# First half of attention in a two-layer MLP kernel: the values of both batches stand together ahead of both results, and the first weight block is loaded and converted later

## The chip, the cores and the metric

The kernel runs on one core of a Trainium2 chip. The metric is the device time of one execution in microseconds (us); less is better. The engines are TensorE (PE, whose weight loads show as PEld), VectorE (DVE), ScalarE (ACT), GpSimd (POOL) and SyncE (SP), which here only issues loads and stores.

## The reference

Three stages follow each other. Attention with a per-head decay runs over 2 batches, 8 heads, 768 tokens of width 64; its result, 1536 rows of 512, goes through a gated MLP of width 1536, and that result through a second MLP of width 768 with three branches. The reference's weights are 64-bit floats.

```python
for b in range(nb):                       # blocks of tokens
    intra = einsum('bhic,bhjc->bhij', qb, kb) * Dmask
    intra = einsum('bhij,bhjd->bhid', intra, vb)
    inter = einsum('bhid,bhde->bhie', qb * lam_pow, kv_state)
    out[:, :, sl] = intra + inter
    kv_state = lam_block * kv_state + einsum('bhsd,bhse->bhde', kb * rev_pow, vb)
x = out.transpose(0, 2, 1, 3).reshape(B * S, H * D)
y = ((x @ w_a) * (x @ w_b)) @ w_out
return maximum(maximum(y @ w1, y @ w2), y @ w3) @ w_out2
```

## The kernel before, in words

**Attention.** The tokens are cut into chunks of 128. `order` (L343) numbers the 12 chunks so that 2m and 2m + 1 are the same chunk of the two batches: `pair(m)`. The first half of the tokens is pairs 0, 1 and 2. Each chunk n goes through these helpers:

- `load` (L357): one 512 KB load for queries and keys (`aq`), one for keys and values in row order (`av`).
- `scores` (L367): on PE, query times key into two banks `s`; `masked` (L377): two DVE passes that multiply a bank by the decay table into `am`.
- `queries` and `keys` (L389, L393): one POOL pass each, which weights `aq` or `av` by the decay.
- `earlier` (L402): on PE, queries times the held state, into the banks `ob` (named `o` in rows). A pair of chunks shares these two banks.
- `within` (L414): on PE, `am` times the values, into the same banks `o`, added to what stands there.
- `update` (L427): on PE, keys times values into a bank `k`; `carry` (L440) takes it into the held state, `stt` in rows: one ACT copy after pair 0, four DVE passes (L448) after the others.
- `taken` (L458): ACT passes that copy the result out of `o`, into `x` (32-bit) and `xh` (the rounded part that PE multiplies with); `lows` (L469): two DVE passes that form the rest, `xl` = `o` - `xh`.

A tile is one unit to the dependency tracker, and both chunks of a pair write one pair of banks `o`. So in program order a `within` that follows a `taken` and a `lows` of the pair's other chunk waits until both have read the banks.

**Weights.** Weight blocks come as 64-bit floats, 1 MB each (`wr`). `converted` (L211) makes 32-bit floats of them in four passes: DVE L221, ACT L224 (`ws`), DVE L229, DVE L231. `up_pair` (L236) then splits the block into `hi` (ACT, L190) and `lo` = `w` - `hi` (DVE or POOL, L187). Block 0 and block 1 belong to the first two column groups of the first MLP; each is six such steps. A `Task` holds the steps of a block; `steps(task, n)` (L838) puts the next n steps into the program there and then, and a task that is on the list `pace.tasks` is also put forward by `pace.pump`, which looks at an estimate of each engine's clock whenever PE work is added. The engine of `lo` is picked by that estimate or named by the third argument of `steps`.

**First MLP.** `plain_group` (L557, matmuls at L567, bank `p`) multiplies `xh`, `xl` by `hi`, `lo` in three terms. Its first group needs `xh`, `xl` of pairs 0 to 2 of batch 0 and `hi`, `lo` of block 0. From there on the other three pairs of attention are threaded between the groups of layer 1 (L915 to L950).

**Order of the work.** The scheduler is off (`manual_schedule`, L744): each engine runs its instructions in the order of the program text, and a wait holds up all that stands behind it on that engine. SP issues loads in text order too. Nine matmuls on zeros (`keep_warm`, L759) open PE's work, and eight more stand between the scores of pair 0 and the first `within`.

Of the kernel before, what the change touches and what calls it, by code (L numbers as in the profile page):

```python
# [163 lines left out]
def decay_attention_gated_mlps(ctx: ExitStack, tc: tile.TileContext, qkv: bass.AP, lam: bass.AP, wup: bass.AP, wdown: bass.AP, out: bass.AP):  # L164
# [7 lines left out]
    pace = Pace()  # L172
# [7 lines left out]
    def bank(name):  # L180
        return pp.tile([128, 512], F32, tag="ps", name=name)
# [17 lines left out]
    def load_to(n):  # L199
        while state["raw"] <= min(n, len(items) - 1):  # L200
            m = state["raw"]
            kind, i = items[m]
            t = wp.tile([128, 1024], I64, tag="r", bufs=2, name=f"wr{m}")
            if kind == "up":
                nc.sync.dma_start(out=t, in_=wup[i])
            else:
                nc.sync.dma_start(out=t[:, 0:WB], in_=wdown[i])
            raw[m] = t
            state["raw"] += 1
# [24 lines left out]
    wop, wtask = {}, {}  # L234
# [67 lines left out]
    def open_to(what, m):  # L302
        if m < len(items):
            items_to(m)
            pace.open((what, m))
# [39 lines left out]
    am, sc, ob, kv, at = {}, {}, {}, {}, {"st": 0.0}  # L345
    xa, xh, xl = {}, {}, {}
# [4 lines left out]
    def arrive(us):  # L351
        state["dma"] += us
        return state["dma"]
# [3 lines left out]
    def load(n, *which):  # L357

        b, c = order[n]
        for i in which:  # L360
            of, name = ((aq, "aq"), (av, "av"))[i]
            of[n] = slot(f"{name}{n}")
            at[name, n] = arrive(1.3)
            s = slice(512 if i == 1 and c == NC - 1 else 0, 1024)
            nc.sync.dma_start(out=of[n][:, s], in_=qkv[b * NC + c, i, :, s])

    def scores(n):  # L367

        q, k = aq[n][:, 0:512], aq[n][:, 512:1024]
        sc[n] = [bank(f"s{n}_{i}") for i in range(2)]  # L370
        for a in range(NP):
            o = slice(128 * a, 128 * a + 128)
            for i in range(2):
                nc.tensor.matmul(sc[n][i][:, o], k[rows(i), o], q[rows(i), o], start=True, stop=True)  # L374
        pace.pe(0.9, at["aq", n])

    def masked(n):  # L377

        am[n] = slot(f"am{n}")
        for i in range(2):  # L380
            nc.vector.tensor_tensor(out=am[n][:, 512 * i:512 * i + 512], in0=sc[n][i], in1=decay[:, 4 * i:4 * i + 4].rearrange("p a i -> p (a i)"), op=ALU.mult)
            at["am", n] = pace.run("DVE", 512, pace.t["PE"])
        sc.pop(n)
# [9 lines left out]
    def keys(n):  # L393
        k, o = (av[n][:, x:x + 512].rearrange("p (h d) -> p h d", h=H) for x in (0, 1024))
        nc.gpsimd.tensor_tensor(out=o, in0=k, in1=decay[:, :, C - 1:C].to_broadcast([128, H, D]), op=ALU.mult)
        at["kd", n] = beside(512, at["av", n])
# [5 lines left out]
    def earlier(n):  # L402

        q = aq[n][:, 1024:1536]
        for w in range(2):
            for i in range(2):
                for x in range(2):
                    a = 2 * w + x
                    nc.tensor.matmul(  # L409
                        place(n, 4 * i + a), held[rows(i), n % 2, a], q[rows(i), 128 * a:128 * a + 128],  # L410
                        start=n % 2 == 0 and w == 0, stop=False, skip_group_check=True)
        pace.pe(0.5, max(at["qs", n], at["st"]))

    def within(n):  # L414

        v = av[n][:, 512:1024]
        for w in range(2):
            for i in range(2):
                for x in range(2):
                    a = 2 * w + x  # L420
                    h = 4 * i + a
                    nc.tensor.matmul(  # L422
                        place(n, h), v[:, 64 * h:64 * h + 64], am[n][:, 128 * h:128 * h + 128],
                        start=n == 0 and w == 0, stop=n % 2 == 1 and w == 1, skip_group_check=True)
        pace.pe(0.9, max(at["av", n], at["am", n]))

    def update(n):  # L427

        if n % 2 == 0:
            kv[n // 2] = bank(f"k{n}")  # L430
        v, k = av[n][:, 512:1024], av[n][:, 1024:1536]
        for a in range(NP):
            for i in range(2):
                h, o = 4 * i + a, 256 * (n % 2) + 64 * a
                nc.tensor.matmul(  # L435
                    kv[n // 2][rows(i), o:o + 64], k[:, 64 * h:64 * h + 64], v[:, 64 * h:64 * h + 64],
                    start=n % 2 == 0 and a == 0, stop=n % 2 == 1 and a == NP - 1, skip_group_check=True)
        pace.pe(0.5, at["kd", n])

    def carry(m):  # L440

        src = kv[m].rearrange("p (b a e) -> p b a e", b=B, a=NP)
        if m == 0:
            copy(held, src)
            at["st"] = pace.run("ACT", 512, pace.t["PE"])
        else:
            for a in range(NP):
                nc.vector.scalar_tensor_tensor(out=held[:, :, a], in0=held[:, :, a], scalar=ahead[:, a, C - 1:C], in1=src[:, :, a], op0=ALU.mult, op1=ALU.add)  # L448
                at["st"] = pace.run("DVE", 128, pace.t["PE"] if a == 0 else 0.0)
# [8 lines left out]
    def taken(n, *to):  # L458
        b, c = order[n]
        j = c // 3  # L460
        for x, name, dt in zip((xa, xh, xl), ("x", "xh", "xl"), (F32, F32R, F32R)):
            if (j, b) not in x and (j == 0 or x is xa):
                x[j, b] = slot(f"{name}{j}{b}", dt).rearrange("p (a i) -> p a i", a=KD)
        for x in to:
            for i in range(2):
                copy(tokens_of(x, n, i), result(n, i))
                at["x", n, i] = pace.run("ACT", 256, pace.t["PE"])

    def lows(n):  # L469
        for i in range(2):  # L470
            nc.vector.tensor_tensor(out=tokens_of(xl, n, i), in0=result(n, i), in1=rd(tokens_of(xh, n, i)), op=ALU.subtract)  # L471
            pace.run("DVE", 256, at["x", n, i])
# [271 lines left out]
    with tc.manual_schedule():  # L744
        nc.sync.dma_start(out=lams, in_=lam)
        for m in range(3):
            for i in range(2):
                for n in (2 * m, 2 * m + 1):
                    load(n, i)
                if m == i == 0:  # L750
                    load_to(0)
                    at["wr"] = arrive(2.6)
        warm = sttab[:, 768:1024].bitcast(BF16)
        nc.vector.memset(warm, 0.0)
        patterns()
# [3 lines left out]
        def keep_warm(n):  # L759
            for i in range(n):  # L760
                nc.tensor.matmul(ps, warm[:, 0:128], warm, start=True, stop=True)
# [76 lines left out]
        def steps(task, n, e=None):  # L838
            while n and task.next is not None:
                if e is None:  # L840
                    task.step(pace)
                else:
                    task.ready = pace.run(e, task.next[1], after=task.ready, kind=task.next[2])
                    task.move(e)
                n -= 1
                pace.gone(task)

        def pair(m):
            return 2 * m, 2 * m + 1
# [11 lines left out]

        open_to("conv", 0)
        open_to("split", 0)
        for n in pair(0):
            scores(n)
            masked(n)
        keep_warm(8)
        wtask[0].ready = at["wr"]
        steps(wtask[0], 5)
        for n in pair(0):  # L870
            keys(n)
        for f, m in ((queries, 1), (keys, 1), (queries, 2)):
            for n in pair(m):
                f(n)
        steps(wtask[0], 1, "POOL")
        for n in pair(2):
            keys(n)
        load_to(1)
        arrive(2.6)
        for i in range(2):  # L880
            for n in pair(3):
                load(n, i)
        for m in range(2):
            ob[m] = [bank(f"o{m}_{i}") for i in range(2)]
            if m > 0:
                for n in pair(m):
                    earlier(n)
            for n in pair(m):
                within(n)
                update(n)  # L890
                taken(n, xh, xa)
                if n < 3:
                    lows(n)
            carry(m)
            for n in pair(m + 1):
                scores(n)
                masked(n)
        for i in range(2):
            for n in pair(4):
                load(n, i)  # L900
        ob[2] = [bank(f"o2_{i}") for i in range(2)]
        for n in pair(2):
            earlier(n)
        for n in pair(2):
            within(n)
            taken(n, xh)
        lows(4)
        lows(3)
        lows(5)
        for n in pair(2):  # L910
            taken(n, xa)
        open_to("conv", 1)
        open_to("split", 1)
        operands(0)
# [130 lines left out]
```

## Time and profile before

| | us |
|---|---|
| runs without profile | 518.37, 518.88, 519.06 (median 518.88) |
| the profiled execution, its own time | 519.24 |
| its span, first to last instruction | 517.5 |
| PE busy in the span | 503.0 (97%) |
| DVE, ACT, POOL busy | 372.5, 213.2, 57.1 |
| stretch 0 to 35.4, before the first MLP matmul | 6.8% of the span |

The profile was taken in one execution. Its page gives busy times of each engine, the span in 40 slices of 12.9 us, and the chain of work that ended last; the trace behind it gives instructions in order of time, each with the idle time of its engine before it and what ended that. PE's busy time cannot tell how well PE is used: a matmul at a low clock is busy for longer. [...]

### The profile page before, as it was taken

The page shows a single profiled execution, that of the slowest core. Times are in us where ns is not written, and L with a number is a line of the kernel's source. Part 1 is how long each engine was busy: PE and PEld are TensorE (multiplying, and loading weights), DVE is VectorE, ACT ScalarE, POOL GpSimd, SP SyncE. Part 2 cuts the span into 40 slices and gives each one's busy share as a digit, 9 for nine tenths or more (in the row PEclk, how much of TensorE's full clock was granted, in tenths as well). Part 3 has the DMA queues.
Part 4 walks back from the last instruction along what each step waited for, and adds up shares of the span by engine and source line. Part 5 has one row for each costly group of instructions (what it writes and reads, how often), then busy time and mean ns, then how long its engine had stood idle before and what let it go on. Part 6 is the DMA issues. An engine that isn't in the chain of part 4 may idle for free.

```text
span 517.5 us, 7772 instructions
## 1 busy us (share of the span) xinstructions
PE 503.0 (97%) x3175; PEld 467.7 (90%) x3175; DVE 372.5 (72%) x555; ACT 213.2 (41%) x358; POOL 57.1 (11%) x50
## 2 busy tenths in 40 slices
PE   6589999999999999999999999999999999999997
PEld 3579999999999999997888888899999999998886
DVE  5655978879777778859958068697999998887000
ACT  2333254534443334445534166354464354433211
POOL 2836210111111111211000000000000000000000
PEclk9799999999999999999999999999999999999999
DMA  8994202022122212303424020202102211110311
GB/s 321 411 345 186 84 2 81 1 81 101 65 81 82 81 63 62 120 5 122 134 79 155 1 81 2 82 1 81 47 37 81 82 61 62 61 62 1 112 70 62
DMA packets 10260, 47.17 MB, mean 91 GB/s; under 512 B 1264, under 2 KB 1520, under 8 KB 7536
## 3 DMA queue, kind: packets, MB, share of 16 engines
q1 hardware_dynamic: 10224, 46.67, 24.5%
q8 instruction: 25, 0.41, 0.3%
q14 instruction: 11, 0.09, 0.1%
HBM read 43.52 MB, written 3.15 MB: 90 GB/s over the span
## 4 chain that ended last, share of the span: by engine, by line
PE 93%; DVE 3%; DMA 1%; ACT 1%; issue 1%; SPq 0%; DVEq 0%
PE yp L666 18%; PE zu L549 16%; PE zv L549 15%; PE out L720 10%; PE bu L549 8%; PE bv L549 7%; PE p L567 6%; PE xu L549 4%; PE xv L549 4%; PE o L422 2%; PE s L374 2%; DMA wr<-wup_dram 1%; PE o L409 1%; PE k L435 1%; DVE gl L187 1%
## 5 line engine op out<-in xcount | busy, mean ns | idle before, releaser
L187 DVE TENSOR_TENSOR lo<-w,hi 128x1024 fp32r<-128x1024 f32 (+1 forms) x39 | 47.5, 1217 | 11.5 <-ACT hi L190 11.5
L190 ACT ACTIVATE hi<-w 128x1024 fp32r<-128x1024 f32 (+1 forms) x40 | 38.2, 956 | 17.5 <-DVE w L231 7.7
L666 PE MATMUL yp<-gl,dh 128*128 128x512 f32 x108 | 42.0, 389 | 0.0
L666 PE MATMUL yp<-gh,dl 128*128 128x512 f32 x108 | 42.0, 389 | 0.0
L666 PE MATMUL yp<-gh,dh 128*128 128x512 f32 x108 | 42.0, 389 | 0.0
L598 POOL TENSOR_TENSOR g<-z1u,z6u 128x384 f32<-128x384 f32 x20 | 24.0, 1202 | 150.3 <-DVE z6u L580 150.3
L187 DVE TENSOR_TENSOR gl<-g,gh 128x512 fp32r<-128x512 f32 x36 | 24.6, 706 | 17.8 <-ACT gh L190 17.8
L187 DVE TENSOR_TENSOR w<-w 128x256 f32<-128x256 f32 (+1 forms) x57 | 29.7, 521 | 1.0
L229 DVE SCALAR_TENSOR_TENSOR w<-ws,w 128x1024 int32<-128x1024 int32 x21 | 26.5, 1261 | 3.1 <-ACT ws L224 3.0
L709 DVE COPY ob<-out 128x256 f32<-128x256 f32 x1 | 0.4, 424 | 38.4 <-PE out L720 38.4
L224 ACT ACTIVATE ws<-wr 128x1024 f32<-128x1024 f32 x21 | 24.1, 1147 | 6.6 <-DMA wr<-wup_dram 6.6
L231 DVE SCALAR_TENSOR_TENSOR w<-ws,w 128x1024 int32<-128x1024 int32 x21 | 26.3, 1254 | 0.3
L190 ACT ACTIVATE z6u<-zu 128x384 f32<-128x384 f32 x20 | 9.8, 492 | 38.2 <-PE zu L549 38.2
L190 ACT ACTIVATE gh<-g 128x512 fp32r<-128x512 f32 x36 | 21.2, 622 | 7.1 <-PE yp L666 7.1
L666 PEld LDWEIGHTS yp<-gh,dl 128*128 128x128 f32 x108 | 20.3, 188 | 4.2
L666 PEld LDWEIGHTS yp<-gh,dh 128*128 128x128 f32 x108 | 20.3, 188 | 4.2
L666 PEld LDWEIGHTS yp<-gl,dh 128*128 128x128 f32 x108 | 20.3, 188 | 4.2
L190 ACT ACTIVATE z7u<-zu 128x384 f32<-128x384 f32 x20 | 9.8, 492 | 34.3 <-PE zu L549 34.3
L422 PE MATMUL o<-am,av 128*64 128x128 f32 x192 | 14.1, 291 | 7.9 <-DVE xl L471 6.1
L221 DVE TENSOR_SCALAR w<-wr 128x1024 int32<-128x1024 int32 (+1 forms) x26 | 18.5, 713 | 2.9 <-DMA wr<-wup_dram 2.5
L549 PE MATMUL zu<-x1A,hi 128*128 128x384 f32 x80 | 20.3, 334 | 0.0
L549 PE MATMUL bu<-x0S,hi 128*128 128x384 f32 x80 | 20.3, 334 | 0.0
(202 smaller groups left out, 1450.0 us busy)
## 6 DMA issues: line engine op xcount, KB each, us to landing
wr<-wup_dram SPq DMA_DIRECT2D x21, 1024.0 KB, 4.8
wr<-wdown_dram SPq DMA_DIRECT2D x12, 768.0 KB, 4.4
aq<-qkv_dram SPq DMA_DIRECT2D x12, 512.0 KB, 10.0
av<-qkv_dram SPq DMA_DIRECT2D x10, 512.0 KB, 10.2
out_dram<-ob SPq DMA_DIRECT2D x11, 256.0 KB, 2.1
av<-qkv_dram SPq DMA_DIRECT2D x2, 256.0 KB, 4.3
out_dram<-ob SPq DMA_DIRECT2D x2, 128.0 KB, 1.7
lams<-lam_dram SPq DMA_DIRECT2D x1, 6.0 KB, 1.6
```

What stands on the lines that cost most here:

```text
L187: (nc.vector if e == "DVE" else nc.gpsimd).tensor_tensor(out=o, in0=a, in1=b, op=op)
L190: nc.scalar.activation(out=o, in_=a, func=AF.Copy)
L221: nc.vector.tensor_scalar(out=w, in0=low, scalar1=29, scalar2=None, op0=ALU.logical_shift_right)
L224: nc.scalar.activation(out=near, in_=high.bitcast(F32), func=AF.Copy, scale=2.0 ** -112)
L229: nc.vector.scalar_tensor_tensor(out=w, in0=near, scalar=3, in1=w, op0=ALU.logical_shift_left, op1=ALU.bitwise_or)
L231: nc.vector.scalar_tensor_tensor(out=w, in0=near, scalar=-0x80000000, in1=w, op0=ALU.bitwise_and, op1=ALU.bitwise_or)
L422: nc.tensor.matmul(place(n, h), v[:, 64 * h:64 * h + 64], am[n][:, 128 * h:128 * h + 128], start=n == 0 and w == 0, stop=n % 2 == 1 and w ...
L549: nc.tensor.matmul(ps, w, x, start=p in FIRST and i == 0, stop=i == len(todo) - 1, skip_group_check=p not in FIRST)
L567: nc.tensor.matmul(ps, w[:, 128 * k:128 * k + 128], x[:, k], start=m == 0, stop=m == 11)
L598: nc.gpsimd.tensor_tensor(out=ga[g.n][:, tokens(g.j, 0)], in0=g.z[1], in1=g.z[6], op=ALU.mult)
L666: nc.tensor.matmul(ps[e], w[:, cols], g, start=k == 0 and m == 0, stop=k == K1 - 1 and m == 2)
L720: nc.tensor.matmul(ps, a[:, o:o + 128], w[:, s], start=k == 0 and n == 0, stop=k == K2 - 1 and n == 2)
```

## The change

Only the first half of attention is written anew (pairs 0 to 2), in the body under `manual_schedule`, and the order of the first loads. Everything up to there, all helpers, and everything from `open_to("conv", 1)` (L912) on are as before. Block 0's task is taken off the list of tasks, so that only `steps` puts its passes into the program.

```diff
             for i in range(2):
                 for n in (2 * m, 2 * m + 1):
                     load(n, i)
-                if m == i == 0:
-                    load_to(0)
-                    at["wr"] = arrive(2.6)
+            if m == 0:
+                load_to(0)
+                at["wr"] = arrive(2.6)
...
+        first = wtask[0]
+        pace.tasks.remove(first)
+        first.ready = at["wr"]
         for n in pair(0):
             scores(n)
             masked(n)
-        keep_warm(8)
-        wtask[0].ready = at["wr"]
-        steps(wtask[0], 5)
-        for n in pair(0):
             keys(n)
-        for f, m in ((queries, 1), (keys, 1), (queries, 2)):
...
-        for m in range(2):
+        for m in range(3):
             ob[m] = [bank(f"o{m}_{i}") for i in range(2)]
             if m > 0:
                 for n in pair(m):
                     earlier(n)
+            if m < 2:
+                for n in pair(m + 1):
+                    queries(n)
+            if m == 0:
+                for n in pair(1):
+                    keys(n)
+            if m == 1:
+                steps(first, 1)
             for n in pair(m):
                 within(n)
-                update(n)
-                taken(n, xh, xa)
-                if n < 3:
-                    lows(n)
-            carry(m)
-            for n in pair(m + 1):
-                scores(n)
-                masked(n)
+            for n in pair(m):
+                taken(n, xh)
+            for n in pair(m):
+                lows(n)
+            if m < 2:
+                for n in pair(m):
+                    update(n)
+                if m == 1:
+                    steps(first, 1)
+                carry(m)
+                if m == 0:
+                    steps(first, 3)
+            for n in pair(m):
+                taken(n, xa)
+            if m == 1:
+                steps(first, 1, "POOL")
+                for n in pair(2):
+                    keys(n)
+                load_to(1)
...
+            if m < 2:
+                for n in pair(m + 1):
+                    scores(n)
+                    masked(n)
```

On the engines the change moves instructions in three places; apart from them, the eight matmuls that are gone, the load of block 0 (now behind both first `av` loads instead of ahead of them) and ACT's passes, the five engines run the same instructions in the same order as before.

PE, the results of pair 0 (`within` L422, `update` L435), before and then after; av_85 and av_87 were the values of chunks 0 and 1, they are now av_83 and av_85:

```order
L422 MATMUL o_0_196<-am_147,av_85 64x128 x2
L422 MATMUL o_1_197<-am_147,av_85 64x128 x2
...
L435 MATMUL k_206<-av_85 64x64 x8
L422 MATMUL o_0_196<-am_160,av_87 64x128 x2
L422 MATMUL o_1_197<-am_160,av_87 64x128 x2
...
L435 MATMUL k_206<-av_87 64x64 x8
```

```order
L422 MATMUL o_0_160<-am_142,av_83 64x128 x2
L422 MATMUL o_1_161<-am_142,av_83 64x128 x2
...
L422 MATMUL o_0_160<-am_156,av_85 64x128 x2
L422 MATMUL o_1_161<-am_156,av_85 64x128 x2
...
L435 MATMUL k_196<-av_83 64x64 x8
L435 MATMUL k_196<-av_85 64x64 x8
```

Both chunks' values now stand together, and both updates behind them; pair 1 moved in the same way.

DVE, from the decay tables to the decay passes (`am`) of pair 1, before and then after; w and lo belong to block 0, xl to the results of pair 0:

```order
L221 TENSOR_SCALAR w_142<-wr_83 128x1024
L229 SCALAR_TENSOR_TENSOR w_142<-ws_144,w_142 128x1024
L381 TENSOR_TENSOR am_147<-s_0_132,tables 128x512
...
L381 TENSOR_TENSOR am_160<-s_1_151,tables 128x512
L231 SCALAR_TENSOR_TENSOR w_142<-ws_144,w_142 128x1024
L187 TENSOR_TENSOR lo_173<-w_142,hi_172 128x1024
L471 TENSOR_TENSOR xl_217<-o_0_196,xh_216 128x2x128
...
L381 TENSOR_TENSOR am_260<-s_0_250,tables 128x512
```

```order
L381 TENSOR_TENSOR am_142<-s_0_132,tables 128x512
...
L381 TENSOR_TENSOR am_156<-s_1_147,tables 128x512
L471 TENSOR_TENSOR xl_184<-o_0_160,xh_183 128x2x128
...
L221 TENSOR_SCALAR w_214<-wr_87 128x1024
L229 SCALAR_TENSOR_TENSOR w_214<-ws_216,w_214 128x1024
L381 TENSOR_TENSOR am_233<-s_0_223,tables 128x512
...
L381 TENSOR_TENSOR am_246<-s_1_237,tables 128x512
L231 SCALAR_TENSOR_TENSOR w_214<-ws_216,w_214 128x1024
```

Two of block 0's DVE passes moved behind the `am` and `xl` of pair 0, ahead of the `am` of pair 1; the third moved behind these; `lo` left DVE.

POOL, from the queries of pair 2 on, before and then after; lo_460 is the `lo` of block 1, lo_271 that of block 0:

```order
L390 TENSOR_TENSOR aq_97<-aq_97,tables 128x512
L390 TENSOR_TENSOR aq_99<-aq_99,tables 128x512
L395 TENSOR_TENSOR av_101<-av_101,tables 128x512
L395 TENSOR_TENSOR av_103<-av_103,tables 128x512
...
L395 TENSOR_TENSOR av_194<-av_194,tables 128x512
L187 TENSOR_TENSOR lo_460<-w_438,hi_459 128x1024
```

```order
L390 TENSOR_TENSOR aq_97<-aq_97,tables 128x512
L390 TENSOR_TENSOR aq_99<-aq_99,tables 128x512
L187 TENSOR_TENSOR lo_271<-w_214,hi_270 128x1024
L395 TENSOR_TENSOR av_101<-av_101,tables 128x512
L395 TENSOR_TENSOR av_103<-av_103,tables 128x512
```

The `lo` of block 0 came to POOL, ahead of the keys of pair 2; that of block 1 left POOL for DVE, where it stands between the `am` and the state's passes of pair 3.

## Rows read from the trace of the kernel before

**Rows 1.** The page's 40 slices of 12.9 us: the granted clock in tenths.

```profile
PEclk9799999999999999999999999999999999999999
```

**Rows 2.** Busy time by stage: start:end length, PE, PEld, DVE, ACT, POOL, PEclk, DMA share, GB/s.

```profile
10.60:14.00 3.40, 1.78 (x32) 1.40 (x32) 3.40 (x6) 0.00 (x0) 3.40 (x3) 1.00 1.03 413
14.00:19.10 5.10, 0.00 (x0) 0.00 (x0) 3.98 (x4) 2.15 (x5) 5.10 (x4) 0.83 1.03 410
19.10:24.20 5.10, 5.04 (x54) 4.89 (x56) 1.26 (x4) 1.84 (x5) 5.07 (x5) 0.51 1.02 412
24.20:35.40 11.20, 10.12 (x208) 8.72 (x204) 6.62 (x14) 3.17 (x11) 4.66 (x4) 1.00 0.97 378
35.40:72.40 37.00, 36.35 (x483) 33.01 (x481) 27.51 (x48) 14.56 (x31) 13.66 (x9) 1.00 0.33 119
72.40:517.50 445.10, 441.51 (x2357) 415.58 (x2357) 324.37 (x469) 188.87 (x305) 24.05 (x20) 1.00 0.19 67
```

**Rows 3.** The chain of work that ended last, up to the first MLP: start, length, what.

```profile
11.29 2.39 DVE am L381 x4
...
19.16 1.98 PE o L422 x16
...
21.98 3.03 PE s L374 x32
...
29.56 0.46 PE k L435 x16
30.02 1.99 PE s L374 x32
...
33.04 0.83 PE o L422 x12
...
35.72 0.43 DVE xl L471
...
36.20 4.26 PE p L567 x23
```

**Rows 4.** PE in order of time: start, length, what, idle before and its end.

```profile
6.30 2.41 PE L374 MATMUL s<-aq 64*128 64x128 f32 x32
...
19.16 1.98 PE L422 MATMUL o<-am,av 128*64 128x128 f32 x16 [5.27 <-DVE xl L471]
```

**Rows 5.** DVE in order of time, in the same form.

```profile
8.87 0.69 DVE L221 TENSOR_SCALAR w<-wr 128x1024 int32<-128x1024 int32 x1 [2.46 <-DMA wr<-wup_dram]
10.06 1.23 DVE L229 SCALAR_TENSOR_TENSOR w<-ws,w 128x1024 int32<-128x1024 int32 x1 [0.50 <-ACT ws L224]
...
13.60 1.93 DVE L231 SCALAR_TENSOR_TENSOR w<-ws,w 128x1024 int32<-128x1024 int32 x1
...
18.69 0.74 DVE L471 TENSOR_TENSOR xl<-o,xh 128x256 fp32r<-128x256 f32 x2
...
49.73 1.12 DVE L448 SCALAR_TENSOR_TENSOR stt<-stt,tables,k 128x128 f32<-128x128 f32 x4 [3.54 <-PE k L435]
...
52.57 1.38 DVE L221 TENSOR_SCALAR w<-wr 128x1024 int32<-128x1024 int32 x1
54.06 2.12 DVE L229 SCALAR_TENSOR_TENSOR w<-ws,w 128x1024 int32<-128x1024 int32 x1
```

**Rows 6.** ACT (its first row) and POOL in order of time.

```profile
26.91 0.66 ACT L190 ACTIVATE xh<-o 128x256 fp32r<-128x256 f32 x2 [4.28 <-PE o L422]
...
13.19 3.48 POOL L390 TENSOR_TENSOR aq<-aq,tables 128x512 f32<-128x512 f32 x2
...
43.47 2.40 POOL L187 TENSOR_TENSOR lo<-w,hi 128x1024 fp32r<-128x1024 f32 x1 [11.82 <-ACT hi L190]
45.83 2.50 POOL L390 TENSOR_TENSOR aq<-aq,tables 128x512 f32<-128x512 f32 x2
```

**Rows 7.** SP's issue of pair 1's queries, and the first one's time to landing.

```profile
3.62 0.99 SPq L365 DMA_DIRECT2D aq<-qkv_dram x2
...
aq<-qkv_dram SPq DMA_DIRECT2D x1, 512.0 KB, 9.1
```

More of the change, by code (lines that the diff above doesn't have):

```diff
@@ L866, in decay_attention_gated_mlps @@
             masked(n)
-        keep_warm(8)
-        wtask[0].ready = at["wr"]
-        steps(wtask[0], 5)
-        for n in pair(0):
             keys(n)
-        for f, m in ((queries, 1), (keys, 1), (queries, 2)):
[L873 to L882, printed above, removed]
-        for m in range(2):
+        for m in range(3):
             ob[m] = [bank(f"o{m}_{i}") for i in range(2)]
@@ L887, in decay_attention_gated_mlps @@
                     earlier(n)
+            if m < 2:
[6 more added lines that the diff above has]
+                steps(first, 1)
             for n in pair(m):
                 within(n)
-                update(n)
-                taken(n, xh, xa)
-                if n < 3:
-                    lows(n)
-            carry(m)
-            for n in pair(m + 1):
-                scores(n)
-                masked(n)
+            for n in pair(m):
[17 more added lines that the diff above has]
+                load_to(1)
+                arrive(2.6)
+                for i in range(2):
+                    for n in pair(3):
+                        load(n, i)
+            if m < 2:
+                for n in pair(m + 1):
+                    scores(n)
+                    masked(n)
         for i in range(2):
@@ L900, in decay_attention_gated_mlps @@
                 load(n, i)
[L901 to L911, printed above, removed]
         open_to("conv", 1)
```

## The prediction

> **What bounds the kernel now.** I read the 40 slices first, then the busy times by stage, then the chain of waits, and last the engines in order of time. [...] The stages [rows 2] say where time can be won: after 72.4 us PE is busy for 441.5 of 445.1 us, from 35.4 to 72.4 for 36.35 of 37.0, all at full clock. Whatever starts these stages earlier moves the end by as much; nothing else in them is touched. Before 35.4 us it is otherwise: PE does nothing from 14.0 to 19.1, and from 19.1 to 24.2 it is busy at 0.51 of the clock.
>
> My landmark is the second matmul of the first MLP, at 36.20 us, the last that waits in this stretch (for `xl`); its chain is in [rows 3]. The wait of 5.27 us ahead of it belongs to the second chunk's `within` [rows 4]: it may not touch the banks `o` until the first chunk's `xl` has read them, and on DVE that `xl` stands behind block 0's third pass (13.60, 1.93 us) and `lo`, and starts only at 18.69 [rows 5]. So a weight block that no product needs before 36 us holds up attention, and the idle time is followed by a low clock: 16 matmuls of `within` in 1.98 us, scores of a pair in 3.03 against 1.99 later [rows 3].
>
> **The change, step by step.** I rebuild the chain to the landmark from rows, handing over between engines at about 0.04 us (from `xl`'s end at 36.15 to the matmul at 36.20, [rows 3]).
>
> 1. *Scores of pair 0* stay at 6.30, 2.41 us for 32 matmuls [rows 4]. The eight matmuls on zeros behind them go; PE then waited for `am`, which began only at 11.29 [rows 3], so by themselves they cost nothing. What they may do for the clock is a rival below.
> 2. *`am` of pair 0*, four passes, 2.39 us from the first start to the last end as the chain counts them [rows 3]. DVE was free from 6.4 (8.87 less the idle 2.46, [rows 5]) and now takes them first: from about 7.8, when half the scores are done, to 10.2. Before, they ended at 13.7.
> 3. *Values of both chunks* follow pass by pass; behind the last pass remain 12 matmuls, 0.83 us [rows 3]: 11.0. The values must have landed for it: they move ahead of the 1 MB block, and at 413 GB/s [rows 2] 1 MB is 2.5 us and 512 KB 1.3; the block now being the last ahead of the load that lands at 12.7 (step 5), the second chunk's values land at 8.9, the first's at 7.6. Updates, 2 x 0.46: 12.0.
> 4. *`xh`, then `xl`.* ACT passes are 0.38 long and 0.28 apart (two in 0.66, [rows 6]). I let `xl` begin after three of them, since it now stands behind both chunks' `xh`: 0.94, then four DVE passes, 2 x 0.74 less an overlap of 0.08 twice, 1.33. `xl` ends at 13.3.
> 5. *Scores of pair 1* need queries issued at 3.62 that land 9.1 us later, at 12.7 [rows 7], the second chunk's one load after that (1.3 us, 512 KB at the same rate): done at 15.0. This load does not move, since what is ahead of it in the queue has the same bytes as before.
> 6. *Block 0's first two DVE passes* now stand ahead of `am` of pair 1. Alone they take 0.69 and 1.23, while POOL works on them, 1.38 and 2.12 [rows 5]. POOL gets its four passes for pair 1 as the loads land, 1.3 us apart from 12.7 on, so I take the dear values, 3.5 us: 16.8. The passes are now what is late, by 1.8 us against the scores.
> 7. *`am` of pair 1* 2.39: 19.2. *Third pass of block 0*, between POOL's passes as before, 1.93: 21.1. `xl` of pair 1, 1.33: 22.5 (`within` ends at 20.0, so `xh` is there). State passes, four in 1.12, next one starting 0.08 before their end: 23.5 (the updates end at 21.0). `am` of pair 2, 2.39: 25.9; its scores (1.99, from 21.0) are done by 23.0.
> 8. *Values of pair 2*, 0.83, *three `xh`*, 0.94, *first `xl`*, 0.43, and three hand-overs, 0.12: the landmark comes at 28.3 instead of 36.2, **7.9 us earlier**.
>
> Costed at nothing: `lo` of block 0 on POOL, 2.40 alone [rows 6], with `hi` ready near 22.5 it is done by 25, ahead of the products; the keys of pair 2 that queue behind it end by 27, and their updates come only after 24 products (some 4.3 us from 36.20, [rows 3]). `lo` of block 1 on DVE stands where DVE idled 3.54 us for an update [rows 5]. Other loads keep their order; pair 3's land before 31 us at this rate and are needed 5 us after the landmark.
>
> The profiled execution took 519.24 us, 1.7 more than its span, and 0.36 more than the median 518.88 of the runs. 519.24 - 7.9 is 511.3 for an execution like it; against the median I say **511.0**.
>
> **Bounds of what I can't see.** Step 6 and 7's three passes never stood in this place. Cheapest, without POOL in their way, they take 0.69, 1.23 and 1.23, 2.3 us less than I took: 508.7. Dearest by rows is what I took; the row nearest is POOL's, whose two query passes took 3.48 beside the third pass and 2.50 alone [rows 6], so I stay there.
>
> [...]
>
> **Rivals.**
>
> *The clock drops in the new stretch.* From 8.6 to 20 PE works in pieces between DVE passes, and the eight filling matmuls are gone. Against it: from 10.6 to 14.0 PE was busy for 1.78 of 3.40 us, and from 24.2 to 35.4 with pauses, at 1.00; the fall came only after 14.0 [rows 2], with PE wholly idle. My longest pause is about 1.5 us. At half clock until the scores of pair 2 are through, two `within` tails cost 0.83 more each, two updates 0.92 and one pair of scores 1.04: 3.6 us, gain 4.3, **514.6**.
>
> [...]
>
> *Slower: the clock stays low into the products.* The same with the third `within`, 4.4 us of the gain gone, and every product then takes 0.185 us longer (4.26 for 23, [rows 3]). After 19 products nothing is left of the gain, and it decides from there; low until 45 us it would lose 6 us on products: **521.5**. But PE is dense from the first product on, and from 19.1, dense, the clock was back by 24.2 [rows 2].
>
> *The passes meet no POOL work,* as bounded: 508.7 to 510.
>
> *The move does not act:* if the values stayed late or some other reader held the banks, `within` of the second chunk would still wait, and block 0's passes would only have changed place: 518 to 519.5.
>
> **How the numbers follow.** Forecast, gain 7 to 9: 0.72. Cheaper passes, over 9: 0.10. Low clock for part or all of attention, gain 3.5 to 7: 0.13. No effect: 0.02. Slower: 0.03. The range runs from 509.0 to 514.7: cheap passes nearly whole, and the low clock up to the scores of pair 2; what is left out is under 0.1 above and about as much below. A measurement can tell 0.2%, 1 us, from no change; all but the last two cases are past it: faster 0.95, same 0.02, slower 0.03.
>
> **What would show it.** Right: the wait of 5.27 gone from PE's rows, the first slices at clock 1.00 once it has risen, `am` of pair 0 from about 7.8, the first two passes of block 0 taking about 3.5 us together and directly ahead of `am` of pair 1, the first product near 27.5 and the second near 28.3, the last two stages as long as before. Wrong in step 6 if these passes take under 2.5; wrong in step 3 if `within` waits for `av`; the forecast falls if the clock shows 0.5 beyond 10 us, or if a stall turns up after the landmark, at the first use of block 1 above all.

## The result, and the profile after

| | before | changed |
|---|---|---|
| median of the runs, us | 518.97 (518.37 to 519.72, 4 runs) | 511.26 (510.32 to 511.82, 4 runs) |
| the profiled execution, its own time | 519.24 | 511.27 |
| span | 517.5 | 509.5 |

The ratio is 0.9849, with a 95% interval of 0.9829 to 0.9869. The forecast was 511.0 for the median, and 7.9 us for the gain between two profiled executions; that gain is 519.24 - 511.27 = 7.97.

The page's slices of the changed kernel, the granted clock in tenths of the full one (written 1.00 in the other views); the dip of [rows 1] is gone:

```profile
PEclk9999999999999999999999999999999999999999
```

Busy time by stage, changed kernel, columns as in [rows 2]; the last two stretches are cut 7.9 us sooner than there:

```profile
14.00:19.10 5.10, 4.09 (x78) 3.39 (x78) 5.00 (x7) 1.22 (x5) 5.10 (x4) 1.00 1.03 413
19.10:24.20 5.10, 5.10 (x116) 4.86 (x114) 4.80 (x11) 3.36 (x9) 5.10 (x4) 1.00 1.02 414
...
27.50:64.50 37.00, 36.08 (x482) 32.94 (x481) 28.90 (x47) 14.67 (x31) 18.81 (x13) 1.00 0.50 197
64.50:509.50 445.00, 441.44 (x2357) 415.51 (x2357) 324.36 (x469) 188.75 (x305) 23.72 (x20) 1.00 0.19 67
```

The clock is 1.00 in every stretch, and the last two stretches are as long as before with PE busy for nearly the same time (36.35 and 441.51 there). The whole gain therefore lies ahead of the first MLP, as forecast. PE of the changed kernel in order of time, in the form of [rows 4]:

```profile
6.30 2.67 PE L374 MATMUL s<-aq 64*128 64x128 f32 x32
8.90 2.63 PE L422 MATMUL o<-am,av 128*64 128x128 f32 x32
...
13.80 2.45 PE L374 MATMUL s<-aq 64*128 64x128 f32 x32 [1.34 <-DMA aq<-qkv_dram]
16.18 0.67 PE L409 MATMUL o<-aq,stt 64*64 64x128 f32 x16
17.73 0.67 PE L409 MATMUL o<-aq,stt 64*64 64x128 f32 x16 [0.89 <-POOL aq L390]
18.33 1.97 PE L422 MATMUL o<-am,av 128*64 128x128 f32 x32
...
28.15 0.44 PE L567 MATMUL p<-xl,hi 128*128 128x384 f32 x1 [0.57 <-DVE xl L471]
```

The wait of 5.27 us [rows 4] is gone and the longest pause left between PE's first result and the first MLP is 1.34. The landmark, the second product, came at 36.20 [rows 3] and comes at 28.15. DVE in the same stretch:

```profile
8.12 2.48 DVE L381 TENSOR_TENSOR am<-s,tables 128x512 f32<-128x512 f32 x4 [1.67 <-PE s L374]
12.33 1.42 DVE L471 TENSOR_TENSOR xl<-o,xh 128x256 fp32r<-128x256 f32 x4 [1.73 <-ACT xh L190]
13.66 0.68 DVE L221 TENSOR_SCALAR w<-wr 128x1024 int32<-128x1024 int32 x1
14.45 2.10 DVE L229 SCALAR_TENSOR_TENSOR w<-ws,w 128x1024 int32<-128x1024 int32 x1
16.48 2.47 DVE L381 TENSOR_TENSOR am<-s,tables 128x512 f32<-128x512 f32 x4
18.87 1.93 DVE L231 SCALAR_TENSOR_TENSOR w<-ws,w 128x1024 int32<-128x1024 int32 x1
21.10 1.42 DVE L471 TENSOR_TENSOR xl<-o,xh 128x256 fp32r<-128x256 f32 x4 [0.30 <-ACT xh L190]
```

Where [rows 5] show `xl` at 18.69, behind the third pass and `lo`, the first `xl` now starts at 12.33, ahead of all of block 0. The chain that ended last, in the middle of this stretch:

```profile
12.67 1.09 DVE xl L471 x3
...
13.80 3.89 POOL aq L390 x2
...
17.73 0.67 PE o L409 x16
18.40 1.70 PE o L422 x28
...
20.13 0.94 ACT xh L190 x3
```

This is not the road that the forecast drew. Between 13.8 and 17.7 the chain runs not through DVE's two passes themselves but through POOL's two query passes, which took 3.89 us beside L229, against 2.50 alone [rows 6]. They begin at 13.80, when their load landed: PE's scores of that chunk begin at the same moment, and its row names the load. POOL's own row names the `xl` that ended at 13.75, but that is not what it waited for: in the second execution (below) POOL begins at 13.47, before `xl` ends at 13.60, and names the load. Block 0's passes still count, by way of POOL.

### The profile page after: what moved, and what is told of

It reads as the page before. It is cut to its first block, busy times and chain, and to the rows that moved or that the text cites. A ratio compares the mean times of both kernels' runs of the same rounds, so it can differ in the third digit from the quotient of the medians.

```text
span 509.5 us, 7757 instructions
## 1 busy us (share of the span) xinstructions
PE 499.7 (98%) x3167; PEld 465.2 (91%) x3167; DVE 373.1 (73%) x555; ACT 212.9 (42%) x358; POOL 59.2 (12%) x50
## 4 chain that ended last, share of the span: by engine, by line
PE 93%; DVE 3%; ACT 1%; POOL 1%; issue 1%
PE yp L666 18%; PE zu L549 16%; PE zv L549 15%; PE out L720 10%; PE bu L549 8%; PE bv L549 7%; PE p L567 6%; PE xu L549 4%; PE xv L549 4%; PE o L422 2%; PE s L374 2%; DVE am L381 1%; PE warm_ps L761 1%; POOL aq L390 1%; PE o L409 1%; DVE gl L187 1%
## 5 line engine op out<-in xcount | busy, mean ns | idle before, releaser
L190 ACT ACTIVATE hi<-w 128x1024 fp32r<-128x1024 f32 (+1 forms) x40 | 38.3, 957 | 12.7 <-DVE w L187 4.7
L187 DVE TENSOR_TENSOR gl<-g,gh 128x512 fp32r<-128x512 f32 x36 | 24.7, 707 | 17.8 <-ACT gh L190 17.8
L229 DVE SCALAR_TENSOR_TENSOR w<-ws,w 128x1024 int32<-128x1024 int32 x21 | 26.7, 1271 | 1.9 <-ACT ws L224 1.7
L231 DVE SCALAR_TENSOR_TENSOR w<-ws,w 128x1024 int32<-128x1024 int32 x21 | 27.1, 1289 | 0.3
L549 PE MATMUL zu<-x1S,hi 128*128 128x384 f32 x80 | 20.3, 334 | 0.0
L549 PE MATMUL bu<-x1S,hi 128*128 128x384 f32 x80 | 20.3, 334 | 0.0
```

Of the source, the lines that this page charges most:

```text
L187: (nc.vector if e == "DVE" else nc.gpsimd).tensor_tensor(out=o, in0=a, in1=b, op=op)
L190: nc.scalar.activation(out=o, in_=a, func=AF.Copy)
L229: nc.vector.scalar_tensor_tensor(out=w, in0=near, scalar=3, in1=w, op0=ALU.logical_shift_left, op1=ALU.bitwise_or)
L231: nc.vector.scalar_tensor_tensor(out=w, in0=near, scalar=-0x80000000, in1=w, op0=ALU.bitwise_and, op1=ALU.bitwise_or)
L549: nc.tensor.matmul(ps, w, x, start=p in FIRST and i == 0, stop=i == len(todo) - 1, skip_group_check=p not in FIRST)
```

## The experiments

Beside the time each run is read at the landmark (36.20 before, 28.15 changed), since several differences are too near 0.2% for medians to tell. A landmark comes from one profiled execution; the changed kernel's second has it at 28.71, so a difference of about 0.6 between two landmarks can come from the execution alone. "Ratio" is against the kernel before, with its 95% interval.

**The regrouping alone.** The kernel before, with only the order inside the pairs changed; loads, fill and block 0 as before.

```diff
                 within(n)
-                update(n)
-                taken(n, xh, xa)
-                if n < 3:
-                    lows(n)
-            carry(m)
+            for n in pair(m):
+                taken(n, xh)
+            for n in pair(m):
+                lows(n)
+            if m < 2:
+                for n in pair(m):
+                    update(n)
+                carry(m)
...
```

> The kernel before, with only the order of each pair changed in the first half: values of both chunks, then rounded results of both, rests of both, updates. Block 0's passes stay in a lump ahead of the decay passes, loads and the fill stay. Theory of the forecast (bank wait and placed passes both count): the decay passes still end at 13.7 on DVE, the values at about 14.5, then DVE does the third pass and the lo (to 18.8) and only then the rests and the decay passes of pair 1; PE idles about 3 us there, and the clock may fall as before. Landmark at 30 to 32.5 us, so 4 to 6 of the 8 us; time 513 to 515. Rival (placing the passes singly carries it all): landmark at 35 or later. Rival (the bank wait is all of it): landmark at 28 to 29.

Measured: 514.39 us (514.25 to 515.55), ratio 0.9909 [0.9891, 0.9928]; landmark 31.13. PE's first results in this run:

```profile
11.81 3.75 PE L422 MATMUL o<-am,av 128*64 128x128 f32 x32 [2.19 <-DVE am L381]
15.39 1.10 PE L435 MATMUL k<-av 128*64 128x64 f32 x32
```

The wait of 5.27 is gone, although `xl` still stands behind the third pass and `lo` and starts at 18.56. So it was the shared banks that made the second `within` wait. What stays late is `am` of pair 1, which starts at 19.89 (16.48 in the changed kernel). The regrouping alone is worth 5.1 us at the landmark.

**The placing alone.** The changed kernel with the old order inside the pairs. For pair 2 it is not quite the old one: the kernel before put both `within` of that pair ahead of its `lows`, this run does not.

```diff
                 within(n)
-            for n in pair(m):
-                taken(n, xh)
-            for n in pair(m):
+                if m < 2:
+                    update(n)
+                taken(n, xh, xa)
                 lows(n)
...
```

> The changed kernel (loads, single passes, no fill) with the old order inside each pair: values, update, both results and rests of one chunk, then of the other. Theory of the forecast: the second chunk's values wait for two rounded results on ACT (0.66 us), two rests on DVE (0.75) and hand-overs, about 1.6 us, in pair 0 and pair 1; part of that hides behind the loads of pair 1 (13.67). Landmark at 29.7 to 31.2 us, so 5 to 6.5 of the 8 us; time 513 to 514.5. [...] Rival (the bank wait carries the gain): landmark at 33 or later.

Measured: 513.62 us (512.43 to 514.79), ratio 0.989 [0.9867, 0.9912]; landmark 30.62. The waits for the banks stay, but short, because nothing of block 0 stands ahead of `xl`:

```profile
11.87 1.21 PE L422 MATMUL o<-am,av 128*64 128x128 f32 x16 [0.81 <-DVE xl L471]
...
18.51 2.14 PE L422 MATMUL o<-am,av 128*64 128x128 f32 x16 [1.95 <-DVE am L381]
20.44 1.07 PE L435 MATMUL k<-av 128*64 128x64 f32 x16
22.01 1.21 PE L422 MATMUL o<-am,av 128*64 128x128 f32 x16 [0.50 <-DVE xl L471]
```

Alone it is worth 5.6 us, and somewhat more without pair 2's order: from pair 2's first `within` to the landmark pass 3.96 us here (26.66 to 30.62), 3.23 in the kernel before (32.97 to 36.20). The clock did not stay at 1.00 as in the changed kernel: behind the pause of 1.95 us it was 0.73 on the mean of the next stretch. The two parts add up to 10.7 where both together give 8.05: either part by itself takes most of the same 5.27 us away.

**The old load order.** The changed kernel with block 0 loaded ahead of the first values again.

```diff
-            if m == 0:
-                load_to(0)
-                at["wr"] = arrive(2.6)
+                if m == i == 0:
+                    load_to(0)
+                    at["wr"] = arrive(2.6)
```

> The changed kernel with the load of block 0 back ahead of the first values. Theory of the forecast: the second chunk's values land one 512 KB load after 10.1, at about 11.4, instead of 9.9; its matmuls then end at about 12.3 instead of 11.3, and everything behind shifts by 1 us at most, less where the queries of pair 1 (13.67) end the wait: landmark 28.5 to 29.5 us, time about 512. Rival (the values loaded ahead carry the gain): the landmark goes back by more than half of the 8 us, to 32 or later, time 515 or more.

Measured: 513.49 us (512.8 to 514.76), ratio 0.989 [0.9867, 0.9913]; landmark 29.78; both lie a little past what was expected. Its stretches and PE's results of pair 1:

```profile
14.00:19.10 5.10, 2.97 (x66) 2.36 (x62) 5.00 (x8) 2.28 (x6) 3.85 (x5) 1.00 1.03 406
19.10:24.20 5.10, 5.00 (x72) 4.64 (x74) 3.94 (x9) 2.71 (x7) 3.81 (x3) 0.67 1.02 414
```

```profile
18.49 0.44 PE L422 MATMUL o<-am,av 128*64 128x128 f32 x4 [1.97 <-DVE am L381]
19.08 2.74 PE L422 MATMUL o<-am,av 128*64 128x128 f32 x28 [0.16 <-DVE am L381]
21.61 1.92 PE L435 MATMUL k<-av 128*64 128x64 f32 x32
```

Behind the pause of 1.97 us the clock fell (0.67 in the next stretch): `within` took 2.74 against the 2.07 of the same 28 matmuls at 1.00 (shown below, in the run with the fill), the updates 1.92 against 1.10. The expectation lacked this: the chain of this run goes through both, where that of the changed kernel's second execution goes on from `am` through DVE. Of the 1.5 us about 0.75 reach the landmark: it comes 9.54 us after `am` of pair 1 is done (20.24), against 8.82 in the changed kernel's second execution (19.89 to 28.71) and 8.78 in the run with the fill (20.40 to 29.18). What the order of the loads does by itself shows in `am` of pair 1, done at 20.2 against 18.95 and 19.89 in the changed kernel's two executions: 0.3 to 1.3 us.

**The fill put back.** The changed kernel with the eight matmuls on zeros again behind the scores of pair 0.

```diff
             keys(n)
+        keep_warm(8)
         for m in range(3):
```

> The changed kernel with the eight matmuls on zeros put back between the scores of pair 0 and the first values. Theory of the forecast (the chain of DVE and PE waits sets the start of the first MLP, the clock follows from it): the eight matmuls took 1.9 us before and stood ahead of a wait for the decay passes until 11.2 us; now those passes start at 8.1, so the fill holds PE until about 10.6 to 10.8, all 32 matmuls of the values (1.75 us at full rate) come after it, end near 12.4 instead of 11.3, and the second matmul of the first MLP comes at about 29.2 us instead of 28.15; time about 512.3. Rival (the clock needs the fill): the clock is granted more than in the changed kernel and the landmark comes earlier than 28.15. It can't show much here, since the changed kernel's clock was 1.00 all through; a landmark at 28.15 would say that the fill is hidden as before.

Measured: 512.1 us (511.81 to 512.69), ratio 0.9861 [0.9841, 0.9881]; landmark 29.18. PE:

```profile
9.18 1.90 PE L761 MATMUL warm_ps<-stt 128*128 128x512 bf16 x8
11.01 1.97 PE L422 MATMUL o<-am,av 128*64 128x128 f32 x32
...
18.66 0.44 PE L422 MATMUL o<-am,av 128*64 128x128 f32 x4 [1.73 <-DVE am L381]
19.26 2.07 PE L422 MATMUL o<-am,av 128*64 128x128 f32 x28 [0.16 <-DVE am L381]
```

The values no longer start at 8.90 but wait for the fill, until 11.01, and the clock is 1.00 with the fill as it is without. So the fill bought nothing here. The landmark is 1.0 later than in the changed kernel's first execution and 0.5 later than in its second (below); the medians do not stand apart.

**The clock held through the wait.** The kernel before, with matmuls on zeros in a bank of their own in the place where PE waited 5.27 us; first 24, then 18 of them.

```diff
             for n in pair(m):
+                if n == 1:
+                    warm2 = bank("warm2_ps")
+                    for _ in range(24):
+                        nc.tensor.matmul(warm2, warm[:, 0:128], warm, start=True, stop=True)
                 within(n)
```

> The kernel before, with 24 more matmuls on zeros, into a bank of their own, between the first chunk's update and the second chunk's within, so that PE is not idle in the stretch from 14 to 19 us; nothing else is moved and no result changes. Theory: the 5.27 us wait itself stays (within of the second chunk starts near 19.2, since DVE is as late as before), but the clock does not fall, so that the within takes about 1.2 instead of 1.98, the scores of pair 1 about 2.0 instead of 3.03 and the updates half; the second product comes at 33.0 to 34.0 instead of 36.20 and the time is 516.0 to 517.0. So of the gain of 7.9 some 2 to 3 us are the clock's and 5 to 6 the wait's. Rival: the low clock was hidden behind DVE, the second product stays within 0.5 of 36.2 and the time within 0.7 of the kernel before.

> As the run with 24 matmuls on zeros, with 18 of them, since the 24 lasted until 20.71 us, 0.8 past the end of xl that the second chunk's within waits for. Theory: from the second within to the second product 14.7 us pass at full clock (20.71 to 35.44 in that run), against 17.04 in the kernel before (19.16 to 36.20); with the within at 19.2 to 20.0 the second product comes at 33.9 to 34.7 and the time is 516.7 to 517.7. So about 2.3 us of the 7.9 are the clock's. Rival: the stretch was shorter only because DVE had got ahead during the fill; then the second product stays at 35.4 or later and the time at 518.4 or more.

Measured: with 24, 518.4 us, ratio 0.9983 [0.9972, 0.9995], landmark 35.44; with 18, 517.63 us, ratio 0.9971 [0.9958, 0.9985], landmark 35.08. The first misses theory and rival, the second meets the theory's time and misses its landmark by 0.4. PE of the run with 18:

```profile
12.88 0.44 PE L422 MATMUL o<-am,av 128*64 128x128 f32 x4 [2.22 <-DVE am L381]
...
15.21 5.21 PE L892 MATMUL warm_ps<-stt 128*128 128x512 bf16 x18
20.34 1.09 PE L422 MATMUL o<-am,av 128*64 128x128 f32 x16
```

Two things made the run with 18 miss. Block 0 landed later, so that DVE began it at 9.80 instead of 8.87 and `xl` came 0.9 later; and the clock had already fallen behind the pause of 2.22 (0.67 from 14.0 to 19.1), so that 18 matmuls took 5.21 us (8 of the same form took 1.90 at 1.00, from 8.76 in this run). In the run with 24 `xl` came 0.5 later, and the matmuls on zeros lasted 0.8 us past it. From the second `within` on the reading is the same in both runs: 20.71 to 35.44 is 14.73 us, 20.34 to 35.08 is 14.74, against 19.16 to 36.20, 17.04, in the kernel before. The difference arises where PE works without a pause: 8.39 us from that `within` on in the kernel before, 6.08 for the same matmuls in the run with 18. So 2.3 of the 7.9 us were the low clock behind the wait. The two runs gained less, 0.8 and 1.1 at the landmark, because their second `within` began 1.6 and 1.2 us later.

**Two of block 0's passes left out.** The changed kernel without L229 and L231 for block 0; that block's weights then lack the bits which these passes add.

```diff
-        nc.vector.scalar_tensor_tensor(out=w, in0=near, scalar=3, in1=w, op0=ALU.logical_shift_left, op1=ALU.bitwise_or)
+        if m > 0: nc.vector.scalar_tensor_tensor(out=w, in0=near, scalar=3, in1=w, op0=ALU.logical_shift_left, op1=ALU.bitwise_or)
...
-        nc.vector.scalar_tensor_tensor(out=w, in0=near, scalar=-0x80000000, in1=w, op0=ALU.bitwise_and, op1=ALU.bitwise_or)
+        if m > 0: nc.vector.scalar_tensor_tensor(out=w, in0=near, scalar=-0x80000000, in1=w, op0=ALU.bitwise_and, op1=ALU.bitwise_or)
```

> The changed kernel without two of block 0's three DVE passes, those that put the last bits into w (L229 and L231); the result is therefore less exact for that block, and the output differs in what these passes add. Theory from the chain of the changed kernel: between 13.8 and 17.7 the chain runs through POOL's two query passes, which take 3.88 us beside L229 and 2.5 alone, while the third pass at 18.87 is hidden behind the wait for xh; so the second product comes 1.0 to 1.6 earlier than its 28.15, at 26.5 to 27.2, and the time is 509.6 to 510.5. Rival, as the prediction added them up: both passes lie on the chain with their 2.10 and 1.93 us, the second product comes at 24.1 to 24.7 and the time is 507.2 to 508.0.

Measured: 509.86 us (509.48 to 510.03), ratio 0.9821 [0.9807, 0.9836]; landmark 26.96. The chain then goes through a load, the values of chunk 3:

```profile
5.28 12.62 DMA av<-qkv_dram
...
18.04 0.89 PE o L422 x12
```

4.0 us of passes gone (2.10 and 1.93) bring 1.2 of landmark against the first execution and 1.75 against the second: directly behind the passes comes the queue of loads, which nothing in the forecast's sum named as next. Landmark and time lie where this run's expectation had them (26.5 to 27.2, 509.6 to 510.5), but the road through the load was not in it.

**The changed kernel again,** together with two other placings.

> The changed kernel once more, as the yardstick of the next run on the same chip: 511.0 to 511.8, second product at 28.0 to 28.7, clock 1.00 all through.

Measured: 511.39 us (510.62 to 512.49), ratio 0.9849 [0.9825, 0.9874]; landmark 28.71. In this execution the chain is nearer to the forecast's own, through DVE's passes:

```profile
13.60 1.70 DVE w L221
...
15.40 2.10 DVE w L229
17.50 2.40 DVE am L381 x4
19.89 0.79 DVE w L231
```

The queries landed 0.3 sooner than in the first execution, so POOL was at work while L221 ran, and it took 1.78 instead of 0.68.

**Block 0's passes later, queries of pair 1 sooner.**

```diff
-            if m == 0:
-                load_to(0)
-                at["wr"] = arrive(2.6)
+                if m == 1 and i == 0:
+                    load_to(0)
+                    at["wr"] = arrive(2.6)
...
-            if m == 1:
-                steps(first, 1)
...
-                if m == 1:
-                    steps(first, 1)
                 carry(m)
-                if m == 0:
-                    steps(first, 3)
+                if m == 1:
+                    steps(first, 2)
...
                     masked(n)
+                if m == 0:
+                    steps(first, 3)
```

> The changed kernel with block 0's first two DVE passes behind the decay passes of pair 1 instead of ahead of them, its third pass behind the state's passes of pair 1, and the queries and keys of pair 1 loaded ahead of block 0. Theory: the chain of the changed kernel passes through POOL's query passes, 3.88 us beside L229 and 2.5 without it, and starts with a load that lands at 13.67; with L229 elsewhere and that load 1 MB sooner in the queue, the earlier results and the second product come 0.5 to 1.5 sooner, at 26.7 to 27.7, and the time is 509.8 to 510.8. Rival: what is moved only meets POOL elsewhere (the keys and lo of block 0), or the products then wait for hi and lo of block 0, which come later: second product at 28.2 to 29.5, time 511.3 to 512.5.

Measured: 510.91 us (510.84 to 511.15), ratio 0.9839 [0.9818, 0.9861]; landmark 27.99. This lies between theory and rival. All three passes now take what they take alone (0.69, 1.23, 1.22), and yet the landmark moves by 0.2 to 0.7 only:

```profile
13.57 1.10 PE L409 MATMUL o<-aq,stt 64*64 64x128 f32 x32
16.64 1.09 PE L422 MATMUL o<-am,av 128*64 128x128 f32 x16 [1.97 <-DMA av<-qkv_dram]
```

`within` of pair 1 waits for its values. Their place in the queue has not changed, since block 0 stands ahead of them in the changed kernel too: the second chunk's landed at 17.8 here, at 18.3 in the changed kernel's first execution. PE merely reaches them sooner. Against the 511.39 beside it, the median is 0.5 lower, too little to tell from no change: no version here that does all the work is shown to beat the changed kernel.

**Block 0's passes sooner.**

```diff
-            if m == 0:
-                load_to(0)
-                at["wr"] = arrive(2.6)
+                    if m == 0 and i == 1 and n == 0:
+                        load_to(0)
+                        at["wr"] = arrive(2.6)
...
             keys(n)
+        steps(first, 3)
         for m in range(3):
...
-            if m == 1:
-                steps(first, 1)
...
-                if m == 1:
-                    steps(first, 1)
                 carry(m)
                 if m == 0:
-                    steps(first, 3)
+                    steps(first, 2)
```

> The changed kernel with block 0's first two DVE passes already behind the decay passes of pair 0, ahead of its lows, and the queries of pair 1 loaded ahead of the values of pair 0. Theory: the passes then lie in the time in which DVE waits for the first values (1.7 us) and mostly ahead of POOL's query passes; second product 27.3 to 28.3, time 510.4 to 511.4, no worse than the changed kernel. Rival: as in the kernel before, a pass that starts late holds up xl and with it all that follows: second product over 29, time over 512, and a pause of PE over 1.9 us with the clock at 0.5 to 0.8 behind it.

In one point the edit does less than this says: the queries of pair 1 are still loaded behind the values of pair 0. What moved is block 0, from behind both values to between them.

Measured: 511.7 us (511.12 to 512.34), ratio 0.9854 [0.9831, 0.9878]; landmark 28.54. Time and landmark end 0.3 and 0.2 past the expectation and are the changed kernel's own; nothing was won, since the second chunk's values now land behind block 0:

```profile
11.90 1.09 PE L422 MATMUL o<-am,av 128*64 128x128 f32 x16 [2.06 <-DMA av<-qkv_dram]
```

The granted clock stayed at 1.00 behind this pause and behind the 1.97 of the run before it.

## Why the prediction was right

The mechanism is the forecast's: the wait on the shared banks went, the passes behind it were spread out, and all of the gain lies ahead of the first MLP. That the first execution's landmark came within 0.15 is in part luck, as steps 5 and 6 show; the second came 0.4 late. By its steps, as forecast, in the first profiled execution and in the second:

| | forecast | first | second |
|---|---|---|---|
| 2, `am` of pair 0 done | 10.2 | 10.60 | 10.45 |
| 4, `xl` of pair 0 done | 13.3 | 13.75 | 13.60 |
| 5, scores of pair 1 done | 15.0 | 16.25 | 15.91 |
| 6, L229 done | 16.8 | 16.55 | 17.50 |
| 7, `am` of pair 1 done | 19.2 | 18.95 | 19.89 |
| 7, `xl` of pair 1 begins | 21.1 | 21.10 | 21.68 |
| 7, `am` of pair 2 done | 25.9 | 25.94 | 26.51 |
| 8, landmark | 28.3 | 28.15 | 28.71 |

*Step 1* holds: without the fill the clock stayed, and the fill put back delayed PE's first results. *Steps 2 to 4* hold, 0.25 to 0.45 late from the start on, because the first scores took 2.67 and 2.53 instead of 2.41. *Step 5* was too early by 1.0: the first queries landed at 13.7, not 12.7. It cost little: in the second execution they landed at 13.3, met L221 instead, and L229 was done later, not sooner.

*Step 6* is right in its sum by a road that it did not draw. It charged 3.5 us of DVE passes under POOL's work. In the first execution the two passes took 2.78, and what was late was POOL; in the second they took 3.88, and DVE was late. Pass by pass (start, length, end, in us):

| first execution | | second execution | |
|---|---|---|---|
| DVE L221 | 13.66, 0.68, 14.34 | POOL L390 | 13.47, 1.28, 14.75 |
| POOL L390 | 13.80, 1.67, 15.47 | DVE L221 | 13.52, 1.78, 15.30 |
| DVE L229 | 14.45, 2.10, 16.55 | POOL L390 | 14.70, 1.72, 16.42 |
| POOL L390 | 15.44, 2.25, 17.69 | DVE L229 | 15.40, 2.10, 17.50 |

Each pass but the first starts before the other engine's pass has ended, and ends 0.55 to 1.14 us after it, a little less than it takes alone. So the passes ran one after the other, to within 0.15 us, and a row's length holds the wait for the other engine. From the first start to the last end it is 4.03 us in both executions; added up alone the four are 0.69 + 1.23 + 2.50 = 4.42. Which engine is late changes from one execution to the next, the total does not. That is why the dear value was nearly right; what should have been summed is the work of both engines in the stretch. In the first execution two errors also met: pair 1's load was 1.0 later than step 5 had it, and DVE's two passes were 0.7 shorter than charged.

The ends of L229 and of POOL's passes around it lie 1.08 to 1.14 us apart. L221 shows the same in the second execution: it ended 0.55 us after POOL's first pass and took 1.78 us against 0.69 alone. The 2.12 us that step 6 took for L229 from [rows 5] stands against 1.23 alone and so holds such a wait already; L229 took 2.10 in both executions.

*Step 7* counts four passes for `xl` of pair 1. One move beside the three named ahead belongs to this: in the kernel before, chunk 3's `xl` stood behind that of chunk 4 (six passes from 35.72), now it stands with chunk 2's. The step also put the third pass on the chain. In the first execution it lay beside it (done at 20.80, while `xl` waited for `xh` until 21.10), in the second on it (19.89 to 21.7), by less than 0.1: the third `xh` was done at 21.6. *Step 8* holds: from `am` of pair 2 to the landmark 2.2 us in both executions, 2.4 in the forecast, whose own terms for it add up to 2.3. `lo` of block 0, costed at nothing, was done on POOL at 25.50 in the first execution, ahead of the products.

Of the rivals, the low clock did not come, but it was nearer than I argued. That the fall came "only after 14.0", with PE wholly idle, was read from one execution with one fall; five runs showed a fall behind pauses of 1.95 to 2.68 us. The changed kernel's longest is 1.34. The price put on it, 3.6 us, was not reached where a fall could be priced at the landmark: about 0.75 in the run with the old load order, 2.3 in the kernel before. The rival in which the move does not act falls with the result, and with the regrouping alone. "Cheaper passes" falls too: where they were cheap (0.69, 1.23, 1.22, with the reordered loads) the values' load took their place. That I did not name: step 3 and step 5 counted the loads of pair 0 and pair 1's queries, but not pair 1's values. In the changed kernel's first execution the first chunk's landed at 17.0 and the second's at 18.27; PE began the first's `within` at 18.33 and came to the second's some 0.9 us later.

## What to carry to other kernels

When two chunks share a tile, put both writers ahead of the first reader; here that alone gave 5.1 of 8 us at the landmark, although the late passes stayed where they were. If two edits each take away the same wait, their gains do not add (5.1 and 5.6 us alone, 8.05 together), so rebuild the chain for both together. Where DVE and POOL passes wait for each other, sum the stretch over both engines (4.03 us in both executions here, whichever engine was late), and name the load that comes next behind them before counting on cheaper passes (4.0 us of passes left out gave 1.2 to 1.75 at the landmark).

## What the runs showed of the hardware

**The clock after short pauses.** PE's longest pause between 9 and 20 us in ten executions, and the lowest mean granted clock of the stretches of [rows 2] from the one that holds it up to 24.2 us (1.00 is the full clock).

| run | pause, us | clock |
|---|---|---|
| changed kernel, first | 1.34 | 1.00 |
| fill put back | 1.73 | 1.00 |
| placing alone | 1.95 | 0.73 |
| old load order | 1.97 | 0.67 |
| passes later | 1.97 | 1.00 |
| passes sooner | 2.06 | 1.00 |
| regrouping alone | 2.19 | 0.69 |
| clock held, 18 | 2.22 | 0.67 |
| clock held, 24 | 2.68 | 0.72 |
| kernel before | 5.27 | 0.51 |

A pause of about 2 us went both ways (two of 1.97: 0.67 and 1.00), so in these runs its length alone does not decide; what does was not tried.

**DVE and POOL passes one after the other.** L221 and L229 on DVE and L390 on POOL ran one after the other in both executions of the changed kernel, to within 0.15 us, although their rows overlap: two passes of each engine took 4.03 us from the first start to the last end, 4.42 added up alone (the table at step 6). `am` (L381) was not slowed by POOL's work: its four passes took 2.47 us beside it (from 16.48 in the changed kernel) and 2.48 with POOL idle (from 12.85 with the passes later; POOL had no pass from 12.91 to 16.57).

**When queued loads land.** In the kernel before and in the changed kernel's first execution most of the first 512 KB loads landed 1.25 to 1.29 us behind the one ahead, but not all: the first values of pair 0 in the changed kernel took 2.67, those of pair 1 2.02. The 1 MB block took 7.60 us from issue to landing in the run with 18 matmuls on zeros, 6.67 in the kernel before, issued at 2.17 in both. From 10.6 to 24.2 us the rate was 410 to 418 GB/s in each stretch of these three runs. So the landing of pair 1's queries, forecast from [rows 7] for the same bytes ahead, was early by 1.0 us in the first execution (13.7 against 12.7).
